# Layernorm, an S5 scan and a gated feed-forward on one core: first up-projection weights loaded and used by whole row tiles, with a new order of all steps

## The chip, the cores and the metric

The kernel runs on one core of a Trainium2 chip. The metric is the device time of one execution in microseconds (us), here the median of three runs: 179.26 before the change.

A core has five engines with a queue of instructions each: TensorE (PE, with the load of its stationary operand shown apart as PEld), VectorE (DVE), ScalarE (ACT), GpSimd (POOL) and SyncE (SP). An engine takes its instructions in the order in which they were written; across engines only semaphores set an order. Nearly all transfers of this kernel are issued by SP, some of them transposing on the way.

## The reference, cut to what matters

```python
def _A_ref(x, Lambda_re, Lambda_im, B_re, B_im, C_re, C_im, log_dt, Dskip):
    Lam = Lambda_re + 1j * Lambda_im
    dt = jnp.exp(log_dt)
    Lam_bar = jnp.exp(dt * Lam)
    B_bar = ((Lam_bar - 1.0) / Lam)[:, None] * Bmat
    Bu = jnp.einsum("bld,pd->blp", x + 0j, B_bar)
    for t in range(L):
        h = Lam_bar[None, :] * h + Bu[:, t, :]
    y = 2.0 * jnp.einsum("blp,dp->bld", hseq, Cmat).real + x * Dskip[None, None, :]

def _B_ref(x, w_gate, w_up, w_down):
    return (_gelu(x @ w_gate) * (x @ w_up)) @ w_down

xn = _layernorm(x, axis=-1)
return x + _A_ref(xn, ...) * _silu(_B_ref(xn, w_gate, w_up, w_down))
```

x is 2048 tokens by 512 in bf16, the state has 512 complex channels, and the feed-forward is 1376 wide.

## The kernel before

**Tiling.** The tokens are four slabs (s) of 512, each four token tiles (m) of 128. The model width is four row tiles (k) of 128. The 1376 columns of the up and gate weights are three chunks (c): 512, 512 and 352 columns. One PE group is the four matmuls over k that fill one PSUM bank for one token tile and one chunk; 16 KB of PSUM per partition are eight banks, six in a pool called `ps` and two in a pool called `pp`.

**The plan.** The kernel's functions don't issue anything directly. Each call puts a step (an engine, a function that emits the instructions, what it reads and writes) into a `Plan`; steps are numbered in the order of the calls. `Plan.run` then emits them in the order of the tuple `ORDER`, written out by hand, and a buffer's or bank's number for each use comes from `SLOTS`, also written out. Costs and due times in the calls ("end", "landed", "rank") play no part in what is emitted. So what the chip sees is, for each engine, the order of its own steps in `ORDER`, and for each buffer who used it last.

**The first slab (s = 0).** `load_x` (L296) and `load_w` (L287) issue the pieces on SP, in `ORDER`'s order: x0, x1, x2 and wu row tile 0, chunk 0; then single row tiles of chunks 0 and 1 of wu (128 KB each) with x3 among them, row tile 3 as 1024 columns, one block with the last 352 columns of all four row tiles, and two blocks of wg. Behind them come slab 1, the skip vector `Drow`, the B matrices by transposing DMA (`BT`), and so on.

`center` (L411 to L424) takes the mean off a token tile with ACT and DVE, `squares` (L428) sums the squares on ACT, and POOL makes the reciprocal deviation `rs`. The mean-free tile is transposed on PE by `head_t` (L387, L400; four transposes a tile) and copied by DVE to `xcT`, which lies in the scan's buffer W. Because `rs` is not yet known, the products are made of the unscaled tile, and ACT scales them while it copies them out of PSUM (`out_up`, L471; for the gate together with the gelu, L505).

`up_rows` (L462) issues a single matmul of an up group, for one m, k and c, so that PE can work on whichever row tile has arrived, with several banks open at once. It is used for chunks 0 and 1 of all token tiles, streaming by row tile. `first_w` (L499) issues a whole group of four; it makes chunk 2 of the up product and the three gate chunks of every token tile. `parameters` (L672, L673) transposes the step sizes and eigenvalues on PE with two small transposes; the DVE, POOL and ACT steps behind them (`angles`, `tables`) make the rotation tables `tab`.

**Later slabs.** ACT normalizes a token tile to `xna` (L843), a transposing DMA on SP makes `xnT` of four tiles (`dma_t4`, L436), and `gate_tile` (L536, copies L539) makes up and gate groups.

**What all slabs share.** The gated product (DVE, L518) overwrites `at`, SP transposes it into `atT` (`at_t`, L551), and `down_pair` multiplies it with `wd` (L564, 11 matmuls of 512 columns) and ACT puts a silu on it (L567). The scan is made in two halves (h) of the channels per slab: four PE groups per half multiply `BT` with `xnT` (L615), ACT copies them to U (L617), DVE rotates them with a table (`rot`, L627, and `turn`, L635 and L639), runs four scans (L646), carries the end state (L655 to L660) and rotates back into `hst`. `y_part` makes an output tile: ACT puts the skip part into a bank (L575), PE adds eight matmuls of `hst` and the scaled C matrices (L579), DVE multiplies by the silu (L585) and adds x (L586), and SP stores it (L589).

**The C matrices** come by two transposing DMAs into `CT` (L807), which lies in slab 1's `hst` buffer; for each of four pieces ACT makes `tF` (L809) and DVE two products (L811, L814) that form C2, the last of which has to stand before the first output product.

**ACT's tables.** Silu and sine stand in one table set and gelu in another; each change of the set that the order brings about puts an ACT_TABLE_LOAD ahead of the step.

**The SP queue in the middle.** Up to the first `atT` its order is: slab 1, `Drow`, `BT` real, xnT(0), `BT` imaginary, slab 2, wd's tail (L763), slab 3, xnT(1), wd (L762), C imaginary, `atT` of tiles 0 and 1 of slab 0, C real.

The two calls by which the change's head goes are these:

```python
        if (m, c) not in opened:
            opened[m, c] = bank(m == 3)
...
            T.matmul(ps[:], lhsT=xcT[:, k, m * P : (m + 1) * P], rhs=wu[:, k, a:b], start=(k == 0), stop=(k == KT - 1))
        pe(1, 512, f, [("xcT", m, k // 2), ("wu", k, c)], [key])
```

Of the kernel before, what the change touches and what calls it, by code (L numbers as in the profile page):

```python
# [51 lines left out]
    ),  # L52
    "pp": (
        0, 1, 0, 1, 0, 1, 0, 1, 0, 0, 0, 1, 0, 1, 0, 1, 0, 1, 0, 1, 1, 0, 1, 0, 1, 1, 1, 0, 0, 0, 0, 1, 1, 0, 1, 0, 1, 0, 1,
    ),
    "U": (
        0, 1, 0, 2, 0, 1, 0, 2,
    ),
    "g2": (
        5, 0, 1, 4, 3, 0, 4, 2, 2, 0, 1, 5, 3, 1, 4, 5,  # L60
    ),
    "at": (
        2, 0, 1, 3, 2, 1, 0, 0, 0, 1, 2, 3, 2, 3, 0, 1,
    ),
    "gtA": (
        0, 0, 1, 1, 0, 1, 0, 1, 1, 0, 0, 0, 1, 1, 0, 0,
    ),
    "gtB": (
        1, 1, 0, 0, 0, 0, 1, 1, 1, 0, 0, 0, 0, 1, 0, 1,
    ),  # L70
    "ubA": (
        0, 1, 0, 0, 1, 1, 1, 0, 0, 0, 1, 1,
    ),
    "ubB": (
        0, 0, 1, 1, 1, 0, 0, 1, 0, 0, 1, 0,
    ),
    "yg": (
        0, 0, 1, 1, 0, 1, 0, 1, 0, 1, 1, 0, 0, 0, 1, 0, 1, 0,
    ),
    "ot": (  # L80
        1, 1, 1, 0, 1, 0, 0, 0, 0, 0, 0, 1, 1, 0, 1, 0, 1,
    ),
    "sk": (
        2, 3, 0, 1, 5, 7, 4, 6, 0, 1, 3, 2, 5, 4, 6, 7,
    ),
    "atT": (
        0, 1, 3, 0, 1, 1, 3, 2, 0, 3, 2, 1, 1, 2, 3, 0,
# [61 lines left out]
def kernel(  # L149
# [18 lines left out]
    P = 128  # L168
    S = 2048
    D = 512  # L170
    F = 1376
# [129 lines left out]
    load_x(2, 2.06, 3.75)  # L301
    load_w("wu", 0, 1, 0, W1, 2.53, 4.4)
    load_w("wu", 0, 1, W1, W2, 3.0, 4.95)
    load_w("wu", 1, 2, 0, W1, 3.47, 5.5)
    load_w("wu", 1, 2, W1, W2, 3.94, 6.05)
    load_x(3, 4.41, 6.6)
    load_w("wu", 2, 3, 0, W1, 4.88, 7.15)
    load_w("wu", 2, 3, W1, W2, 5.35, 7.7)
    load_w("wu", 3, 4, 0, W2, 5.82, 8.8)
    load_w("wu", 0, KT, W2, F, 6.29, 10.0)  # L310
    load_w("wg", 0, KT, W1, F, 6.76, 12.4)
    load_w("wg", 0, KT, 0, W1, 7.23, 14.0)
    for ri, src in enumerate((A_B_re, A_B_im)):
        dma(SP, 2.0, 3.0, lambda ri=ri, src=src: nc.sync.dma_start_transpose(out=BT[:, ri, :, :], in_=src), writes=[("BT", ri)],
            after=list(sp_last), svc=TURN)
    ident = sb("ident", [P, P])
    pool(0.65, lambda: make_identity(nc, ident[:]), writes=["ident"], rank=600.0, not_before=0.72)
# [136 lines left out]
    def up_rows(m, k, c):  # L454

        a, b = CH[c]
        if (m, c) not in opened:
            opened[m, c] = bank(m == 3)
# [461 lines left out]
```

## Time and profile before

| what | us |
|---|---|
| runs | 178.82, 179.26, 179.27 |
| median | 179.26 |
| profiled execution, first to last instruction (its span) | 176.9 |
| mean granted TensorE clock | 1.000 of full speed |

No time of its own was taken for the profiled execution: it has the span alone, and the runs' times are taken around the whole launch, so the two differ by what lies ahead of the first and behind the last instruction. Where a time is predicted, that difference is taken as constant.

Busy time by stretch of the span (us; in brackets instructions), from the view of windows:

| window | PE | DVE | ACT | POOL |
|---|---|---|---|---|
| 0 to 7 | 6.12 (28) | 3.69 (18) | 4.95 (13) | 2.48 (12) |
| 7 to 16 | 8.95 (49) | 3.36 (13) | 7.24 (17) | 3.68 (9) |
| 31 to 71.2 | 39.99 (194) | 38.35 (70) | 39.53 (77) | 1.01 (1) |
| 173.8 to 176.9 | 0.00 (0) | 0.71 (2) | 0.00 (0) | 0.00 (0) |

How to read the rows below. Times are microseconds unless marked ns. `L499` is line 499 of the kernel; `bank<-wu,W` is output and inputs by the program's names (`xcT` appears as W, CT as `hst`). In the chain of waits each row is the start, the length, and the engine with its line: the chain is followed back from the last instruction to what released each step. In a time line a row is the start, the time from the first to the last of a run of equal instructions, the engine, the line, the operation, shapes and their count. A row of windows gives the window, its length, then busy time and count of PE, PEld, DVE, ACT and POOL, the granted clock, the busy share of the DMA engines and the KB per us (GB/s) that they moved. A DMA row gives the mean size and the median time from issue to landing. "issue" stands for time in which nothing that the profile shows was waited for.

### The profile page before, as it was taken

To read this page: it belongs to the slowest core of one execution; us is meant where nothing else is said; L and a number is where in the kernel's file an instruction comes from. 1 tells how busy PE (TensorE), PEld (TensorE's weight loads), DVE (VectorE), ACT (ScalarE), POOL (GpSimd) and SP (SyncE) were. 2 spreads that over 40 slices of the span, in tenths; PEclk is the share of its full clock that TensorE was granted. 3 is DMA by queue.
4 is the path that set the end of the run, shared out by engine and by line. 5 is a ranking of instruction groups with operands and counts; after the bars stand their busy time and mean duration, and the time that the engine had idled before them with its cause. 6 is when DMAs were issued, how large, how long until landed. Compare 5 with 4: busy or idle time off the path is not lost.

```text
span 176.9 us, 2418 instructions
## 1 busy us (share of the span) xinstructions
PE 172.1 (97%) x834; PEld 82.3 (47%) x849; DVE 154.6 (87%) x253; ACT 132.6 (75%) x246; POOL 10.9 (6%) x25
## 2 busy tenths in 40 slices
PE   8999999999999999999999999999999999999992
PEld 2554544454454444444444444444444444444451
DVE  3743799999999988999999699999999999999343
ACT  6679999989999999956697665735898860793310
POOL 2640500000200000011000000000000000000000
PEclk9999999999999999999999999999999999999999
DMA  5999999997092730040057050063007300550531
GB/s 150 285 347 247 160 288 189 305 217 158 8 193 43 138 62 4 0 82 0 0 115 150 2 111 0 0 126 70 0 11 154 87 0 4 129 123 0 113 119 30
DMA packets 48467, 18.66 MB, mean 105 GB/s; under 512 B 40296, under 2 KB 48328, under 8 KB 48456
## 3 DMA queue, kind: packets, MB, share of 16 engines
q1 hardware_dynamic: 48432, 18.52, 46.7%
q8 instruction: 6, 0.10, 0.2%
q14 instruction: 5, 0.04, 0.1%
q10 hardware_dynamic: 24, 0.00, 0.0%
HBM read 6.46 MB, written 2.10 MB: 48 GB/s over the span
## 4 chain that ended last, share of the span: by engine, by line
PE 94%; DMA 2%; SPq 1%; issue 1%; DVE 0%
PE bank L536 31%; PE bank L564 21%; PE bank L615 16%; PE bank L579 16%; PE bank L499 7%; PE bank L462 3%; DMA wu<-in_B_w_up_dram 2%; SPq L296 1%; SPq L287 0%; DVE yg L585 0%; DVE ot L586 0%; PE bank L400 0%
## 5 line engine op out<-in xcount | busy, mean ns | idle before, releaser
L536 PEld LDWEIGHTS <-xnT 128*128 128x128 bf16 x288 | 28.1, 98 | 29.4
L564 PE MATMUL bank<-wd,atT 128*128 128x512 bf16 (+1 forms) x174 | 40.2, 379 | 0.1
L536 PE MATMUL bank<-wu,xnT 128*128 128x512 bf16 (+1 forms) x140 | 31.9, 356 | 0.1
L536 PE MATMUL bank<-wg,xnT 128*128 128x512 bf16 (+1 forms) x139 | 31.7, 356 | 0.3
L615 PE MATMUL bank<-xnT,BT 128*128 128x512 bf16 x128 | 30.9, 379 | 0.1
L646 DVE TENSOR_TENSOR_SCAN Fs<-rho,ini,W 128x512 bf16<-128x512 f32 x24 | 29.8, 1272 | 0.1
L579 PE MATMUL bank<-C,hst 128*128 128x512 bf16 (+1 forms) x134 | 29.7, 366 | 0.1
L564 PEld LDWEIGHTS <-atT 128*128 128x128 bf16 (+1 forms) x176 | 17.2, 98 | 20.3
L539 ACT ACTIVATE ubA<-bank 128x512 bf16<-128x512 f32 x24 | 14.6, 614 | 8.8 <-PE bank L536 8.3
L617 ACT ACTIVATE U<-bank 128x512 bf16<-128x512 f32 x32 | 19.1, 622 | 1.7 <-PE bank L615 1.7
L579 PEld LDWEIGHTS <-hst 128*128 128x128 bf16 x136 | 13.3, 98 | 14.0
L615 PEld LDWEIGHTS <-BT 128*128 128x128 bf16 x128 | 12.5, 98 | 14.3
L627 DVE TENSOR_TENSOR Q<-U,tab 128x4096 bf16<-128x4096 bf16 x8 | 18.3, 2287 | 0.7 <-ACT tab L715 0.6
L539 ACT ACTIVATE gtA<-bank 128x512 bf16<-128x512 f32 x24 | 14.8, 616 | 5.3 <-PE bank L536 4.6
L627 DVE TENSOR_TENSOR Q<-Fs,tab 128x4096 bf16<-128x4096 bf16 x8 | 18.3, 2285 | 0.1
L567 ACT ACTIVATE g<-bank 128x512 f32<-128x512 f32 x16 | 9.2, 594 | 12.1 <-PE bank L564 12.1
L585 DVE TENSOR_TENSOR yg<-bank,g 128x512 bf16<-128x512 f32 (+1 forms) x17 | 11.1, 655 | 5.0 <-PE bank L579 4.6
L539 ACT ACTIVATE ubB<-bank 128x352 bf16<-128x352 f32 x12 | 5.7, 475 | 6.6 <-PE bank L536 5.5
L838 ACT ACTIVATE junk<-x_tok 128x512 bf16<-128x512 bf16 x16 | 10.2, 649 | 0.0
L499 PE MATMUL bank<-wg,W 128*128 128x512 bf16 (+1 forms) x47 | 9.7, 356 | 0.1
L843 ACT ACTIVATE xna<-x_tok,nb,rs 128x512 bf16<-128x512 bf16 x12 | 9.6, 876 | 0.0
L575 ACT ACTIVATE bank<-sk 128x512 f32<-128x512 bf16 (+1 forms) x17 | 9.5, 577 | 0.1
(121 smaller groups left out, 190.0 us busy)
## 6 DMA issues: line engine op xcount, KB each, us to landing
out_dram<-ot SPq DMA_DIRECT2D x15, 128.0 KB, 1.8
x_tok<-in_A_x_dram SPq DMA_DIRECT2D x3, 512.0 KB, 5.6
wd<-in_B_w_down_dram SPq DMA_DIRECT2D x1, 1280.0 KB, 7.1
wg<-in_B_w_gate_dram SPq DMA_DIRECT2D x1, 864.0 KB
wu<-in_B_w_up_dram SPq DMA_DIRECT2D x6, 128.0 KB, 3.3
x_tok<-in_A_x_dram SPq DMA_DIRECT2D x4, 128.0 KB, 2.2
wg<-in_B_w_gate_dram SPq DMA_DIRECT2D x1, 512.0 KB, 7.8
wu<-in_B_w_up_dram SPq DMA_DIRECT2D x1, 352.0 KB, 3.9
```

What stands on the lines that cost most here:

```text
L499: T.matmul(ps[:, 0 : b - a], lhsT=xcT[:, k, m * P : (m + 1) * P], rhs=wt[:, k, a:b], start=(k == 0), stop=(k == KT - 1))
L536: T.matmul(ps[:, 0 : b - a], lhsT=xnT[:, s % 2, m, k, :], rhs=wt[:, k, a:b], start=(k == 0), stop=(k == KT - 1))
L539: acts(b - a, lambda: act(out=dst, in_=ps[:, 0 : b - a], func=AF.Copy if up else AF.Gelu_apprx_tanh), [key], [ok], table=None if up else " ...
L564: T.matmul(ps[:], lhsT=atT[:fs, k, iT * P : (iT + 1) * P], rhs=wd[:fs, k, :], start=(k == 0), stop=(k == NFT - 1))
L579: T.matmul(ps, lhsT=hst[s % 2][:, j // NPT, j % NPT, m * P : (m + 1) * P], rhs=C2[:, j // NPT, j % NPT, c0:c1], start=False, stop=(j == 2 ...
L585: dve(w, lambda: V.tensor_tensor(out=yg[iy][:, 0:w], in0=ps, in1=g2[ig][:, c0:c1], op=ALU.mult), [key, ("g2", gg)], [("yg", gy)])
L615: T.matmul(ps[:], lhsT=BT[:, ri, k, pt * P : (pt + 1) * P], rhs=xnT[:, s % 2, :, k, :], start=(k == 0), stop=(k == KT - 1))
L617: acts(512, lambda q=q, ri=ri, ps=ps: act(out=U[ui][:, ri, q, :], in_=ps[:], func=AF.Copy), [key], [("U", ug, q, ri)])
L627: dve(4096, lambda: V.tensor_tensor(out=Qf, in0=src.unsqueeze(1).to_broadcast(WQ), in1=table, op=ALU.mult), reads, ["Q"], rate=2.0)
L646: pl.add(DVE, 1.12 if s == 0 else 1.185, lambda ri=ri, q=q, pt=pt, first=first: V.tensor_tensor_scan(out=Fs[:, ri, q, :], data0=rho[:, pt ...
L838: acts(512, lambda i=i, fn=fn, sc=sc, m=m: act(out=junk()[:], in_=x_tok[:, s * M + m, :], func=fn, scale=sc, accum_out=sx[:, s, i, m : m + ...
L843: acts(512, lambda m=m: act(out=xn[m], in_=x_tok[:, s * M + m, :], func=AF.Identity, scale=rs[:, s, m : m + 1], bias=nb[:, s, m : m + 1]), ...
```

## The change

**Loads.** Each row tile of wu now comes as two pieces, 512 columns and 864 columns (chunks 1 and 2 together), eight pieces in all; the block with the last 352 columns of all row tiles and the 1024-column piece are gone. In the program the call for x2 stands behind wu(0, chunk 0) and that for x3 behind wu(2, chunks 1 and 2). As `ORDER` issues them: x0, x1, x2, wu(0, 512), wu(0, 864), wu(1, 512), wu(1, 864), wu(2, 512), wu(2, 864), x3, wu(3, 512), wu(3, 864), wg, wg.

**Products of the first slab.** `up_rows` streams all three chunks of token tiles 0 and 1 and chunks 0 and 1 of tile 2, by row tile, and its matmul is as wide as its chunk. Chunk 2 of tile 2 and the whole of tile 3 are made by `first_w`. The banks of tile 2 come from the pool `pp` where those of tile 3 did. The number and the widths of all matmuls together stay the same.

**Orders.** `ORDER` and `SLOTS` are new from the first step to the last. Decoded by engine, what differs most is this.

- PE: the parameters' transposes stand right behind those of token tile 0 and ahead of those of tile 1; behind tile 2's transposes the up matmuls of all three chunks are mixed. Behind the streams come two up groups of tile 3, then gate groups with the last up groups between them: up (3, 0), up (3, 1), gate (0, 2), gate (3, 1), gate (1, 2), gate (3, 0), gate (0, 1), gate (2, 1), gate (3, 2), gate (2, 0), up (3, 2), gate (0, 0), gate (1, 1), the first Bu group, up (2, 2); the number pairs are token tile and chunk. The first output tile is (slab 0, tile 3) where it was (0, 2), with 242 matmuls of 512 columns ahead of it where there were 258.
- SP, behind the loads: slab 1, `Drow`, `BT` imaginary, xnT(0), `BT` real, slab 2, xnT(1), wd's tail, C imaginary, C real, slab 3, wd, then `atT` of slab 0 for tiles 3, 1, 2, 0.
- DVE: ahead of the last C2 piece stand one rotation, one carry and one small gated product less.
- ACT: the order calls for 19 changes of the table set where there were 15.

```diff
 ORDER = (
-    18, 23, 19, 17, 20, 22, 21, 29, 0, 24, 28, 16, 25, 1, 26, 2, 27, 3, 4, 30, 31, 11, 44, 32, 6, 33, 34, 46, 45, 7, 35, 5, 36, 50, 65, 47, 67, 69,
...
+    18, 16, 29, 24, 0, 1, 3, 25, 26, 2, 27, 30, 44, 31, 32, 33, 45, 46, 34, 35, 36, 38, 65, 39, 47, 19, 66, 67, 51, 50, 37, 4, 5, 6, 7, 8, 9, 10,
...
     load_x(0, 1.12, 2.92)
     load_x(1, 1.59, 3.35)
-    load_x(2, 2.06, 3.75)
-    load_w("wu", 0, 1, 0, W1, 2.53, 4.4)
-    load_w("wu", 0, 1, W1, W2, 3.0, 4.95)
-    load_w("wu", 1, 2, 0, W1, 3.47, 5.5)
-    load_w("wu", 1, 2, W1, W2, 3.94, 6.05)
-    load_x(3, 4.41, 6.6)
-    load_w("wu", 2, 3, 0, W1, 4.88, 7.15)
-    load_w("wu", 2, 3, W1, W2, 5.35, 7.7)
-    load_w("wu", 3, 4, 0, W2, 5.82, 8.8)
-    load_w("wu", 0, KT, W2, F, 6.29, 10.0)
-    load_w("wg", 0, KT, W1, F, 6.76, 12.4)
-    load_w("wg", 0, KT, 0, W1, 7.23, 14.0)
+    load_w("wu", 0, 1, 0, W1, 2.06, 3.85)
+    load_x(2, 2.53, 4.3)
+    load_w("wu", 0, 1, W1, F, 3.0, 5.3)
+    load_w("wu", 1, 2, 0, W1, 3.47, 5.75)
+    load_w("wu", 1, 2, W1, F, 3.94, 6.6)
+    load_w("wu", 2, 3, 0, W1, 4.41, 7.05)
+    load_w("wu", 2, 3, W1, F, 4.88, 7.9)
+    load_x(3, 5.35, 8.3)
+    load_w("wu", 3, 4, 0, W1, 5.82, 8.9)
+    load_w("wu", 3, 4, W1, F, 6.29, 9.9)
+    load_w("wg", 0, KT, W1, F, 6.76, 12.6)
+    load_w("wg", 0, KT, 0, W1, 7.23, 14.3)
...
         if (m, c) not in opened:
-            opened[m, c] = bank(m == 3)
+            opened[m, c] = bank(m == 2)
         key, ps = opened[m, c]
 
         def f():
-            T.matmul(ps[:], lhsT=xcT[:, k, m * P : (m + 1) * P], rhs=wu[:, k, a:b], start=(k == 0), stop=(k == KT - 1))
-        pe(1, 512, f, [("xcT", m, k // 2), ("wu", k, c)], [key])
+            T.matmul(ps[:, 0 : b - a], lhsT=xcT[:, k, m * P : (m + 1) * P], rhs=wu[:, k, a:b], start=(k == 0), stop=(k == KT - 1))
+        pe(1, b - a, f, [("xcT", m, k // 2), ("wu", k, c)], [key])
...
     head_t(1)
-    up_rows(0, 0, 0)
-    up_rows(0, 0, 1)
+    for m in range(2):
+        for c in range(3):
+            up_rows(m, 0, c)
     head_t(2)
-    for c in range(2):
-        up_rows(1, 0, c)
-    up_rows(0, 1, 0)
-    up_rows(1, 1, 0)
-    for c in range(2):
-        up_rows(2, 0, c)
-    for m in range(2):
-        up_rows(m, 1, 1)
-    for c in range(2):
-        up_rows(2, 1, c)
+    for k in range(1, KT):
+        for m in range(2):
+            for c in range(3):
+                up_rows(m, k, c)
+        if k == 1:
+            for c in range(2):
+                up_rows(2, 0, c)
+        for c in range(2):
+            up_rows(2, k, c)
     head_t(3)
-    for c in range(2):
-        for m in range(3):
-            up_rows(m, 2, c)
-    for k in range(3):
-        for c in range(2):
-            up_rows(3, k, c)
-    for m in range(M):
-        for c in range(2):
-            up_rows(m, 3, c)
-    for m in range(M):
-        first_w("wu", m, 2)
+    first_w("wu", 2, 2)
+    for c in range(3):
+        first_w("wu", 3, c)
```

More of the change, by code (lines that the diff above doesn't have):

```diff
@@ L48 @@
     "ps": (
[3 rows of a table removed]
[3 rows of a table added]
     ),
     "pp": (
-        0, 1, 0, 1, 0, 1, 0, 1, 0, 0, 0, 1, 0, 1, 0, 1, 0, 1, 0, 1, 1, 0, 1, 0, 1, 1, 1, 0, 0, 0, 0, 1, 1, 0, 1, 0, 1, 0, 1,
+        0, 0, 1, 0, 1, 0, 1, 0, 1, 1, 0, 1, 0, 0, 1, 1, 0, 0, 1, 1, 0, 0, 1, 0, 1, 1, 1, 1, 0, 0, 0, 0, 1, 0, 0, 0, 0,
     ),
     "U": (
-        0, 1, 0, 2, 0, 1, 0, 2,
+        0, 1, 2, 0, 1, 2, 0, 1,
     ),
     "g2": (
-        5, 0, 1, 4, 3, 0, 4, 2, 2, 0, 1, 5, 3, 1, 4, 5,
+        1, 3, 2, 0, 4, 1, 0, 5, 5, 1, 3, 2, 0, 2, 3, 4,
     ),
     "at": (
-        2, 0, 1, 3, 2, 1, 0, 0, 0, 1, 2, 3, 2, 3, 0, 1,
+        2, 1, 0, 3, 1, 2, 0, 3, 0, 2, 3, 1, 3, 2, 1, 0,
     ),
     "gtA": (
-        0, 0, 1, 1, 0, 1, 0, 1, 1, 0, 0, 0, 1, 1, 0, 0,
+        1, 0, 1, 0, 1, 1, 0, 0, 0, 1, 1, 0, 1, 0, 1, 1,
     ),
     "gtB": (
-        1, 1, 0, 0, 0, 0, 1, 1, 1, 0, 0, 0, 0, 1, 0, 1,
+        1, 0, 1, 0, 1, 0, 1, 1, 0, 1, 1, 1, 0, 0, 1, 1,
     ),
     "ubA": (
-        0, 1, 0, 0, 1, 1, 1, 0, 0, 0, 1, 1,
+        1, 1, 0, 1, 1, 1, 0, 0, 1, 1, 1, 0,
     ),
     "ubB": (
-        0, 0, 1, 1, 1, 0, 0, 1, 0, 0, 1, 0,
+        1, 0, 1, 0, 1, 0, 1, 0, 1, 1, 1, 0,
     ),
     "yg": (
-        0, 0, 1, 1, 0, 1, 0, 1, 0, 1, 1, 0, 0, 0, 1, 0, 1, 0,
+        0, 1, 1, 0, 0, 1, 0, 0, 1, 0, 0, 1, 0, 0, 1, 1, 1, 0,
     ),
     "ot": (
-        1, 1, 1, 0, 1, 0, 0, 0, 0, 0, 0, 1, 1, 0, 1, 0, 1,
+        0, 0, 1, 1, 1, 1, 1, 1, 1, 0, 0, 1, 1, 0, 0, 0, 1,
     ),
     "sk": (
-        2, 3, 0, 1, 5, 7, 4, 6, 0, 1, 3, 2, 5, 4, 6, 7,
+        1, 3, 2, 0, 6, 4, 7, 5, 1, 3, 0, 2, 5, 0, 4, 7,
     ),
     "atT": (
-        0, 1, 3, 0, 1, 1, 3, 2, 0, 3, 2, 1, 1, 2, 3, 0,
+        3, 1, 2, 0, 2, 0, 1, 3, 1, 0, 2, 3, 2, 0, 3, 1,
     ),
```

52 rows, old and new, of tables (ORDER, SLOTS) are left out of this document.

## The prediction

> **What bounds the kernel now.** I read the page first, then the chain of waits in order of time, then the time line of the start, and at last those of ScalarE (ACT) and of the SP queue.
>
> ```profile
> span 176.9 us, 2418 instructions
> ```
> ```profile
> PE 172.1 (97%) x834; PEld 82.3 (47%) x849; DVE 154.6 (87%) x253; ACT 132.6 (75%) x246; POOL 10.9 (6%) x25
> ```
> ```profile
> 3.06 3.89 DMA wu<-in_B_w_up_dram
> 6.95 0.04 issue
> 6.99 1.35 PE bank L499 x8
> ...
> 10.24 0.22 PE bank L400 x4
> ...
> 12.40 0.60 PE bank L499 x4
> ...
> 68.10 2.38 PE bank L564 x11
> ...
> 172.01 1.76 PE bank L579 x16
> ```
>
> From 6.99 to 173.77 us the chain is TensorE (PE) alone. Eleven matmuls of 512 columns take 2.38, so one is worth 0.216; four of 352 columns take 0.60, so one is worth 0.15; the four transposes of a token tile take 0.22. The change neither adds nor removes a matmul, so it can win only what PE stands still before 6.99, and it loses whatever new stop it brings behind. What stands behind 173.77, the last product's two DVE steps and its store, keeps its form.
>
> ```profile
> 5.21 0.40 PE L400 MATMUL bank<-ident,xna 128*128 128x128 bf16 x4
> 5.54 0.17 PE L672 MATMUL bank<-ident,pv 4*128 4x4 bf16 x1
> 5.58 0.16 PE L673 MATMUL bank<-ident,pv 8*128 8x8 bf16 x1
> 5.67 1.25 PE L462 MATMUL bank<-wu,W 128*128 128x512 bf16 x5
> 6.99 1.35 PE L499 MATMUL bank<-wu,W 128*128 128x352 bf16 x8
> ```
>
> **The head.** The transposes of token tile 2 start at 5.21; PE is free at 5.43. The next five matmuls start at 5.67, after the parameters' transposes, and at 0.216 apiece are done at 6.75; then PE waits for the 352-column block until 6.99. So 0.24 + 0.24 = 0.48 is lost. In the new order the parameters' transposes stand ahead of token tile 1's, at about 4.3, where PE waits for VectorE (DVE) anyhow, and the 352-column chunks no longer hang on one transfer. What goes is 0.45, if the new pieces land in time.
>
> ```profile
> 2.11 1.93 SPq L287 DMA_DIRECT2D wu<-in_B_w_up_dram  x4
> ```
> ```profile
> x_tok<-in_A_x_dram SPq DMA_DIRECT2D x4, 128.0 KB, 2.2
> ```
> ```profile
> 3.00:6.00 3.00, 2.95 (x20) 1.11 (x18) 2.57 (x10) 2.90 (x10) 0.36 (x2) 1.00 0.90 260
> 6.00:9.00 3.00, 2.94 (x18) 1.54 (x17) 2.25 (x10) 1.61 (x5) 2.67 (x6) 1.00 1.01 298
> ```
>
> SP issues four loads in 1.93, one each 0.475, and by the last column 260 to 298 KB/us arrive. The SP queue still begins with x0, x1, x2, wu(0, chunk 0): the calls are swapped, the order by which they are issued is not. The first new piece, 864 columns or 216 KB, is the fifth. The 352 KB load is issued at 3.06 as the sixth, and lands 3.89 later. The new fifth, issued at 2.58 with fewer bytes, lands at 4.4 (where wu(0, chunk 0) lands: issue at 2.11 plus the 2.2 of a 128 KB tile) plus 216/280 = 0.8, at 5.2; PE wants it at 5.43. The next pieces land 0.45 (128 KB) and 0.77 (216 KB) apart: 5.6, 6.4, 6.9, 7.6, x3 8.1, 8.6, 9.3. PE, counted through its new order, wants them at 6.1, 7.1, 7.4, 8.4, 9.2 and 10.5. The cover is 0.2 for the first piece and 0.5 to 1.2 for the others; gone, it costs what lands late, one for one. I take 0, and up to 0.6 for the range (the third rival).
>
> **ACT's evictions.** PSUM banks are reused as the new slots say, and a matmul group into a used bank waits for ACT's copy out of it.
>
> ```profile
> 9.93 0.71 ACT L428 ACTIVATE junk<-x_tok,ma 128x512 bf16<-128x512 bf16 x1
> ```
> ```profile
> 13.09 0.55 ACT L471 ACTIVATE at<-bank,rs 128x352 bf16<-128x352 f32 x1 [0.19 <-issue]
> ```
> ```profile
> 13.74 1.83 ACT L471 ACTIVATE at<-bank,rs 128x512 bf16<-128x512 f32 x3
> 15.59 1.28 ACT L505 ACT_TABLE_LOAD   x1
> 16.88 0.69 ACT L505 ACTIVATE gtA<-bank,rs 128x512 bf16<-128x512 f32 x1
> ```
> ```profile
> 22.94 2.94 ACT L843 ACTIVATE xna<-x_tok,nb,rs 128x512 bf16<-128x512 bf16 x4
> ```
> ```profile
> 16.00:31.00 15.00, 14.95 (x76) 7.26 (x75) 13.73 (x26) 14.70 (x27) 2.76 (x3) 1.00 1.07 217
> ```
> ```profile
> 71.20:173.80 102.60, 102.08 (x494) 48.96 (x501) 94.78 (x127) 66.13 (x116) 1.01 (x1) 1.00 0.28 60
> ```
>
> Three copies take 1.83, the last of them 0.69: they follow each other every 0.57, 0.12 less than one lasts (so 0.45 or less for 352 columns, which last 0.55); four normalizations take 2.94. From 16 to 31 ACT is busy for 14.70 of 15.00, and PE stays ahead only because each bank it asks for has just been emptied. The new order makes that worse. PE: from 5.48 (tile 2's transposes) 23 matmuls of 512 and 8 of 352 and four transposes, 6.4, to 11.86; two up groups of tile 3 (2 x 0.86), then gate groups (0.60, 0.86, 0.60, 0.86), to 16.50, where gate (tile 0, chunk 1) asks for the bank of gate (3, 1). ACT: its run of copies can start at 11.1, since the cosine ahead waits for DVE; 512, 352, a square (0.71), 352, 512 and 512 columns, to 14.5; the load of the gelu table, 1.28; gate (3, 1) to 16.54. So PE stops for 0.10. Next is tile 2's gate chunk 1 at 17.5, which waits for the copy of up (3, 1), 0.12. At 26.0 gate (1, 0) waits for a copy that stands behind the four normalizations (2.94), 0.12, and the next Bu group another 0.07. At 34.3 an up group of slab 1 waits for a Bu copy that stands behind five sums of slab 2, 0.22. Together 0.63; each comes out of a count of 15 to 25 ACT steps, so 0.2 to 1.2 holds it. I take 0.65.
>
> Counted along the new order ACT changes tables 19 times, where before it is 15: 4 x 1.28 = 5.1 more. All four lie behind 71 us, where ACT is idle for 102.6 - 66.1 = 36.5; there they cost nothing unless a bank hangs on them. Four groups between 73 and 152 keep margins of only 0.1 to 0.25 by my count, for which I add 0.1 (0 to 0.5).
>
> The trace has the first copy behind the load at 16.88, 1.29 after 15.59. [...]
>
> **The SP queue between 25 and 50 us.** Before, the queue runs xnT(1), wd, C_im, two atT, C_re. Now it runs xnT(1), wd's tail, C_im, C_re, slab 3, wd, atT of tile 3, then the other three.
>
> ```profile
> 25.91 2.98 SPq L436 DMA_TRANSPOSE xnT<-xna  x1
> 28.94 0.59 SPq L762 DMA_DIRECT2D wd<-in_B_w_down_dram  x1
> 29.57 6.21 SPq L807 DMA_TRANSPOSE hst<-in_A_C_im_dram  x1
> 35.88 3.13 SPq L551 DMA_TRANSPOSE atT<-at  x2
> 39.06 1.86 SPq L807 DMA_TRANSPOSE hst<-in_A_C_re_dram  x1
> ```
> ```profile
> wd<-in_B_w_down_dram SPq DMA_DIRECT2D x1, 1280.0 KB, 7.1
> ```
> ```profile
> atT<-at SPq DMA_TRANSPOSE x16, 3.5
> ```
>
> wd is issued at 28.94 and lands 7.1 later, at 36.0; the transpose behind it holds SP until 35.78. A transpose behind a big copy thus is stuck until the copy is nearly in. Before, the C transpose stood there; now the first atT does. Its time: xnT(1) is issued at 25.5 (ACT's fourth normalization ends 0.4 earlier) and takes 2.98, to 28.5; the tail 0.5; the two C transposes 1.9 to 2.5 each, to 32.8 to 34.0; slab 3 adds 512 KB ahead of wd, 1.3 to 2.1 at 250 to 400 KB/us; wd 7.1. So wd lands at 41.2 to 43.2 and atT some 2.1 behind (3.5 less the 1.4 that an unhindered issue holds SP): 43.3 to 45.3.
>
> Who waits: DVE's gated product of slab 1, tile 3, which overwrites the buffer that this atT reads. By a count of its steps DVE reaches it at 43.8, and all its later work is queued behind.
>
> ```profile
> 67.31 2.29 DVE L627 TENSOR_TENSOR Q<-U,tab 128x4096 bf16<-128x4096 bf16 x1 [0.64 <-ACT tab L715]
> 69.52 0.74 DVE L811 SCALAR_TENSOR_TENSOR C<-hst,cre,tF 128x512 bf16<-128x512 bf16 x1
> ```
> ```profile
> 71.18 1.89 PE L579 MATMUL bank<-C,hst 128*128 128x512 bf16 x8
> ```
>
> Its due date: the first output product (L579) needs the last of the C2 pieces. Before, that ends at 70.26 and the product starts at 71.18, 0.9 later. In the new order 16 matmuls of 512 fewer stand ahead of the first product (242 for 258): 3.45 earlier, 0.45 earlier from the head, 0.65 later from ACT, so about 67.9. DVE has one rotation (2.2), one carry (0.4) and one small gated product (0.25) less ahead of that piece: 67.4. That leaves 0.4, the wait at 43.8 takes it from 44.2 on, and past it PE loses one for one (at 60.8 a gate group whose bank a silu must empty, then at the product). With atT at 43.3 the loss is 0, at 45.3 it is 1.1; the middle, 44.3, and DVE's usual small waits put it at 0.35.
>
> **Sum.** The profiled execution has a span of 176.9; 2.4 lie around it if it took the median 179.26 (runs: 178.82 to 179.27), and the change touches nothing there. -0.45 + 0.65 + 0.10 + 0.35 = +0.65: a span of 177.5, **179.9**.
>
> **Rivals.** (1) The queue is in time: atT lands before 44.2, and -0.45 + 0.65 + 0 to 0.1 is left, 179.5. For it: 44.2 is inside the bounds. Against: every slip goes one way. (2) The other side, not slower: ACT is never late. It decides at the gate (3, 1) copy: if that ends by 16.4, with the table's load overlapping as at 15.59, the later copies are 0.2 earlier too, all five stops go, and the head's gain stays: 178.8. Against: ACT's 14.70 of 15.00. (3) The loads are late: 864-column rows arrive like the 352-column block, 352 KB from about 4.8 to 6.95, 165 KB/us. Then 216 KB take 1.3, and the pieces come at 5.7, 7.3, 8.9, 10.9; the stops add to 0.6: 180.5. For it: that row; against: 260 to 298 KB/us over the whole stretch. (4) wd is later than 43.2, atT at 45.8, the loss 1.6: 181.1.
>
> **How the numbers follow.** What a measurement of this kernel can tell from no change is about 0.3%, 0.54 us. Forecast 0.37, rivals 0.28, 0.12, 0.13, 0.10. Slower by more than 0.54: most of the forecast (0.33) and of the third and fourth (0.22), 0.55. Faster: half of the second, 0.06. Within: 0.39. The range 178.8 to 181.2 holds all but the ends; the forecast's own is 179.5 to 180.6.
>
> **What would show it.** The 0.24 before 6.99 is gone, and the 352-column up matmuls lie between the others. In the list of waits PE, which now waits for nobody, has ACT behind it at 16 to 18, 26 and 34. The first atT lands at 43.3 to 45.3 and DVE idles before it. Wrong it is if PE's rows run on without a break (rival 2), if SP's copies are not what holds the first atT, or if a stop of over 0.5 stands at a place that I don't name.

## The result, and the profile after

The changed kernel takes 181.67 us (median of four runs, 181.46 to 181.93) against 179.04 (178.76 to 179.27) before: 1.015 times the time, interval 1.013 to 1.017. It is slower, as forecast, but by 2.6 where 0.65 was forecast, and lies above the range.

The chain of waits by engine, before:

```profile
PE 94%; DMA 2%; SPq 1%; issue 1%; DVE 0%
```

The page of the changed kernel, then its list of what PE waited for (in all, times, longest):

```profile
span 180.0 us, 2418 instructions
...
PE 173.2 (96%) x833; PEld 82.4 (46%) x849; DVE 155.0 (86%) x253; ACT 137.9 (77%) x250; POOL 10.4 (6%) x25
...
PE 46%; DVE 32%; ACT 12%; issue 5%; DMA 3%; SPq 0%; ACTq 0%; DVEq 0%
```
```profile
PE bank L564 <- ACT gtA L539: 1.0, 1, 1.0
PE bank L375 <- PEq L896: 0.8, 1, 0.8
PE bank L499 <- ACT gtA L505: 0.7, 1, 0.7
```

The chain is no longer PE alone. Where it now runs through DVE, PE is mostly busy as well, as the windows below show. (The row with L375 is the start of the kernel and is the same before.) The windows answer to those of before:

```profile
16.00:31.00 15.00, 14.29 (x70) 6.79 (x70) 12.82 (x40) 14.99 (x29) 2.51 (x4) 1.00 0.95 177
...
71.20:173.80 102.60, 101.15 (x482) 47.73 (x489) 96.12 (x125) 74.29 (x125) 1.01 (x1) 1.00 0.29 58
```

From 16 to 31 PE is busy for 14.29 where it was for 14.95, and behind 71 us for 101.15 of 102.60.

To place every loss, I went through PE's steps: the start of the next one, less the start of this one, less what this one's matmuls take at full speed (0.2158 per 512 columns, 0.149 per 352, 0.054 per transpose, by the rows of before). What is left is called a **stop** here; it also counts matmuls that run slower. Summed over the trace that is 1.24 before and 4.35 after, 3.11 more; the last product starts 3.08 later (175.80 for 172.72). PE's stops by stretch, in us, with every kernel of this study:

| kernel | to 16 | 16 to 45 | 45 to 140 | 140 on | all | time, us |
|---|---|---|---|---|---|---|
| before | 1.12 | 0.01 | 0.07 | 0.04 | 1.24 | 179.04 |
| before again (e10) | 1.60 | 0.01 | 0.07 | 0.04 | 1.72 | 179.22, one run |
| changed | 1.34 | 1.50 | 0.34 | 1.17 | 4.35 | 181.67 |
| changed again (e11) | 1.70 | 1.48 | 0.10 | 1.17 | 4.44 | 181.88, one run |
| e1, tiny gelu early | 1.57 | 0.54 | 0.50 | 1.18 | 3.80 | 180.88 |
| e2, one wait less | 1.25 | 0.57 | 0.32 | 1.18 | 3.32 | 180.73 |
| e3, tiny gelu late | 1.01 | 1.49 | 0.10 | 0.07 | 2.67 | 180.65 |
| e4, atT first | 1.60 | 1.50 | 0.10 | 1.17 | 4.38 | 181.80 |
| e5, e2 + e3 + e4 | 1.57 | 0.57 | 0.10 | 0.06 | 2.30 | 179.84 |
| e6, e5 + split piece | 1.38 | 0.51 | 0.10 | 0.04 | 2.02 | 179.67 |
| e7, e6 + two moves | 0.96 | 0.49 | 0.10 | 0.04 | 1.58 | 179.51 |
| e12, e7 without split | 1.99 | 0.43 | 0.10 | 0.06 | 2.58 | 179.53 |
| e8, before, parameters first | 1.61 | 0.01 | 0.07 | 0.04 | 1.73 | 178.84 |
| e9, before, row 1 first | 2.54 | 0.01 | 0.07 | 0.04 | 2.66 | 180.06 |

In the changed kernel the 16 to 45 column is 0.82 at 17.95, 0.16 at 18.97, 0.15 at 27.55, 0.07 at 28.48 and 0.30 at 36.02; the 45 to 140 column is 0.13 at 62.45, 0.12 at 74.83 and what any kernel has; the last is 1.14 at 153.54.

### The profile page after: what moved, and what is told of

Same layout as the page of the kernel before. It is cut to its first block, busy times and chain, and to the rows that moved or that the text cites. A ratio compares the mean times of both kernels' runs of the same rounds, so it can differ in the third digit from the quotient of the medians.

```text
span 180.0 us, 2418 instructions
## 1 busy us (share of the span) xinstructions
PE 173.2 (96%) x833; PEld 82.4 (46%) x849; DVE 155.0 (86%) x253; ACT 137.9 (77%) x250; POOL 10.4 (6%) x25
## 4 chain that ended last, share of the span: by engine, by line
PE 46%; DVE 32%; ACT 12%; issue 5%; DMA 3%; SPq 0%; ACTq 0%; DVEq 0%
PE bank L564 14%; PE bank L536 14%; DVE Fs L646 10%; PE bank L579 10%; DVE Q L627 9%; PE bank L615 4%; DVE hst L639 3%; ACT gtA L505 3%; PE bank L462 2%; DVE at L518 2%; DVE W L639 2%; DVE yg L585 2%; DMA wu<-in_B_w_up_dram 2%; PE bank L499 2%; ACT junk L830 2%
## 5 line engine op out<-in xcount | busy, mean ns | idle before, releaser
L564 PE MATMUL bank<-wd,atT 128*128 128x512 bf16 (+1 forms) x171 | 39.6, 379 | 1.2 <-ACT gtA L539 1.0
L536 PE MATMUL bank<-wu,xnT 128*128 128x512 bf16 (+1 forms) x141 | 31.1, 356 | 0.2
L579 PE MATMUL bank<-C,hst 128*128 128x512 bf16 (+1 forms) x132 | 28.7, 366 | 0.2
L539 ACT ACTIVATE ubA<-bank 128x512 bf16<-128x512 f32 x24 | 14.1, 599 | 3.4 <-PE bank L536 3.4
L539 ACT ACTIVATE gtA<-bank 128x512 bf16<-128x512 f32 x24 | 14.2, 613 | 3.0 <-DVE at L518 2.6
L499 PE MATMUL bank<-wg,W 128*128 128x512 bf16 (+1 forms) x47 | 10.2, 356 | 0.7 <-ACT gtA L505 0.7
L830 ACT ACTIVATE junk<-x_tok 128x512 bf16<-128x512 bf16 x16 | 10.7, 687 | 0.0
```

Of the source, the lines that this page charges most:

```text
L499: T.matmul(ps[:, 0 : b - a], lhsT=xcT[:, k, m * P : (m + 1) * P], rhs=wt[:, k, a:b], start=(k == 0), stop=(k == KT - 1))
L536: T.matmul(ps[:, 0 : b - a], lhsT=xnT[:, s % 2, m, k, :], rhs=wt[:, k, a:b], start=(k == 0), stop=(k == KT - 1))
L539: acts(b - a, lambda: act(out=dst, in_=ps[:, 0 : b - a], func=AF.Copy if up else AF.Gelu_apprx_tanh), [key], [ok], table=None if up else " ...
L564: T.matmul(ps[:], lhsT=atT[:fs, k, iT * P : (iT + 1) * P], rhs=wd[:fs, k, :], start=(k == 0), stop=(k == NFT - 1))
L579: T.matmul(ps, lhsT=hst[s % 2][:, j // NPT, j % NPT, m * P : (m + 1) * P], rhs=C2[:, j // NPT, j % NPT, c0:c1], start=False, stop=(j == 2 ...
L830: acts(512, lambda i=i, fn=fn, sc=sc, m=m: act(out=junk()[:], in_=x_tok[:, s * M + m, :], func=fn, scale=sc, accum_out=sx[:, s, i, m : m + ...
```

## The experiments: a table load behind a wait

The two largest stops look alike. The time lines of ACT and of PE in the changed kernel, at 17.95:

```profile
13.10 1.71 ACT L471 ACTIVATE at<-bank,rs 128x352 bf16<-128x352 f32 x3
15.91 1.28 ACT L505 ACT_TABLE_LOAD   x1 [1.11 <-PE bank L499]
17.21 0.69 ACT L505 ACTIVATE gtA<-bank,rs 128x512 bf16<-128x512 f32 x1
```
```profile
17.95 3.51 PE L499 MATMUL bank<-wg,W 128*128 128x512 bf16 x16 [0.66 <-ACT gtA L505]
```

ACT is free at 14.81. The load's row names nothing that it reads, yet it stands still for 1.11, until PE's group is done, and only then takes its 1.28. In before the same load started at once (15.59, behind 13.74 + 1.83), though the last matmul of the group that its copy reads began only at 15.64. The copy behind the load has two waits outstanding in the changed kernel, for PE's group and for POOL's rs of token tile 3, which no ACT step has read yet; in the trace the copy carries one of them, and the other, PE's, stands ahead of it as a semaphore instruction of its own (it ends at 15.88), and ahead of the load, too. In before that copy was of tile 1, whose rs an earlier copy had waited for, and PE's wait stood on the copy alone.

**e1** lets the load start without a wait; **e2** takes one of the two waits away and leaves the load where it was.

```diff
+        def copy():
+            if (m, c) == (3, 1):
+                act(out=tiny[:], in_=one, func=AF.Gelu_apprx_tanh)                 # e1
+                act(out=tiny[:], in_=rs[:, 0, m : m + 1], func=AF.Copy)            # e2, in its place
+            act(out=dst, in_=ps[:, 0 : b - a], func=AF.Gelu_apprx_tanh, scale=rs[:, 0, m : m + 1])
+        acts(b - a, copy, [key, ("rs", 0, m)], [gk], ptr=1, table="gelu", rank=80.0 - 10 * m)
```

> The changed kernel with one tiny gelu on ScalarE, which reads a constant and so waits for nothing, ahead of the copy of gate (3, 1). Theory A: in the changed kernel this copy has two outstanding waits (PE's group and POOL's rs), one of them is put ahead of the table load, and so the load of 1.28 us starts only when PE is done, at 15.91; with the tiny gelu the load starts when the up copies end, at about 14.8, the copy follows PE's group at once, and PE's stop at 17.3 to 17.95 shrinks from 0.82 to about 0.1: the span falls by 0.7, the time from 181.67 to about 181.0. Theory B: ScalarE is full there in any case (14.99 of 15.00 us from 16 to 31), the stop reappears within the next groups: PE's sum of stops by 31 us falls by less than 0.2 and the time stays at 181.5 or above.

> The changed kernel with one tiny copy (no table of its own) on ScalarE that reads rs of token tile 3 ahead of the copy of gate (3, 1); it takes POOL's wait, so that the gelu behind it has PE's wait alone. Theory A (the load is put behind one of two waits): the load carries no wait, starts at about 15.0, and the gain is that of the tiny gelu, 0.6 to 0.7 us: about 181.0. If instead a load always waits with its step, it starts at 15.9 as before and the time stays at 181.7. Theory B (ScalarE is full): 181.5 or above, with the stop moved to later groups.

Measured: 180.88 (180.62 to 181.20) and 180.73 (180.50 to 180.85). The time line of ACT, e1 and then e2:

```profile
13.37 1.71 ACT L471 ACTIVATE at<-bank,rs 128x352 bf16<-128x352 f32 x3
15.09 1.28 ACT L508 ACT_TABLE_LOAD   x1
16.39 0.20 ACT L508 ACTIVATE tiny<-const-float32-1.0 128x1 f32<-128x1 f32 x1
16.50 0.67 ACT L509 ACTIVATE gtA<-bank,rs 128x512 bf16<-128x512 f32 x1
```
```profile
14.74 0.22 ACT L508 ACTIVATE tiny<-rs 128x1 f32<-128x1 f32 x1
14.98 1.28 ACT L509 ACT_TABLE_LOAD   x1
16.28 0.69 ACT L509 ACTIVATE gtA<-bank,rs 128x512 bf16<-128x512 f32 x1
```

In both the load follows its neighbour at once, and the stop of 0.82 is gone, with the next three behind it (0.16, 0.15, 0.07): 16 to 45 falls from 1.50 to 0.54 and 0.57. Theory A holds, and e2 says which half of it counts: with one wait the load runs ahead by itself, at 14.98, where the last matmul of its copy's group begins at 15.45. Theory B falls, by the window of e1:

```profile
16.00:31.00 15.00, 14.90 (x76) 7.17 (x74) 13.47 (x46) 14.99 (x31) 2.92 (x4) 1.00 0.96 181
```

ACT is as full as ever, 14.99, and PE works for 14.90. It was not how much ACT does, but when one load may start. What is left of the stretch are 0.26 (e1) and 0.42 (e2) at 23.1, where the first Bu group waits for xnT(0), and 0.24 and 0.10 at 35.

The second place, ACT, DVE and PE of the changed kernel:

```profile
147.77 1.28 ACT L567 ACT_TABLE_LOAD   x1
149.42 0.60 ACT L567 ACTIVATE g<-bank 128x512 f32<-128x512 f32 x1 [0.36 <-PE bank L564]
151.60 1.28 ACT L539 ACT_TABLE_LOAD   x1 [1.58 <-DVE at L518]
152.90 0.60 ACT L539 ACTIVATE gtA<-bank 128x512 bf16<-128x512 f32 x1
```
```profile
150.84 0.68 DVE L518 TENSOR_TENSOR at<-gtA,ubA 128x1024 bf16<-128x1024 bf16 x1
```
```profile
153.54 2.54 PE L564 MATMUL bank<-wd,atT 128*128 128x512 bf16 x11 [0.97 <-ACT gtA L539]
```

Gate (3, 0) of slab 3 writes a buffer that DVE's gated product reads until 151.52, and it reads PE's bank: two waits again, and the load of 1.28 starts behind DVE's. The load at 147.77 shows the other case: its copy has one wait, for PE, and the load is over at 149.05, before PE's group ends at 149.38. Leaving out the load at the program's start, only the two at 15.91 and 151.60 of the changed kernel's 19 have idle time of more than 0.02 ahead of them; of the 15 of before none has. One load of before, at 110.01, has a semaphore ahead of it as well; that one was passed at 109.42, while ACT was still at work, and cost nothing. **e3** puts a tiny gelu ahead of the copy of gate (3, 0), in the same way as e1.

```diff
+            def copy():
+                if (s, m, nm, c) == (3, 3, "wg", 0):
+                    act(out=tiny[:], in_=one, func=AF.Gelu_apprx_tanh)
+                act(out=dst, in_=ps[:, 0 : b - a], func=AF.Copy if up else AF.Gelu_apprx_tanh)
+            acts(b - a, copy, [key], [ok], table=None if up else "gelu")
```

> The changed kernel with one tiny gelu on ScalarE ahead of the copy of gate (3, 0) of slab 3. Theory A: there the load is put behind the wait for VectorE's gated product (151.52) and the copy ends at 153.49, where PE stands from 152.57 on; with the load done at about 151.3 the copy ends at about 152.15, PE's stop of 1.14 goes, and the time falls by 1.1 to about 180.6. Theory C: the gated product itself, late on VectorE, is what PE hangs on; then PE still stops at this place or at the next group, and at most 0.4 is won: 181.3 or above.

Measured: 180.65 (180.16 to 181.27), 1.0 less. ACT in e3:

```profile
149.48 1.28 ACT L542 ACT_TABLE_LOAD   x1
150.78 0.20 ACT L542 ACTIVATE tiny<-const-float32-1.0 128x1 f32<-128x1 f32 x1
151.07 0.60 ACT L543 ACTIVATE gtA<-bank 128x512 bf16<-128x512 f32 x1
```

The load lies in what was ACT's idle time, the copy follows DVE, and the column "140 on" falls from 1.17 to 0.07. Theory C falls: the product itself was in time.

## The experiments: the SP queue

**e4** puts slab 3 and wd behind the first two atT on SP (steps 438 and 152 behind 177).

```diff
-    ..., 142, 438, 152, 179, 177, ...
+    ..., 142, 179, 177, 438, 152, ...
```

> The changed kernel with the first two atT transposes (token tiles 3 and 1 of slab 0) ahead of slab 3 and wd on SP. Theory D: the transposes stuck behind wd cost VectorE 0.3 to 0.4 at 47.6 to 47.95, and through the sums of slab 2 and a silu PE's stop of 0.13 at 62.4; they now land at about 38 and 41, this idle time and this stop go, and 0.1 to 0.15 us is won (181.5). Rival: VectorE has other waits that take its place (the silu's table load at 60.5), or wd, which lands some 3 us later, holds the first down product; then the time stays at 181.7 or rises.

Measured: 181.80 (181.22 to 182.00), no gain that the time shows. SP and DVE of the changed kernel, then DVE of e4:

```profile
35.68 0.51 SPq L754 DMA_DIRECT2D wd<-in_B_w_down_dram  x1
36.29 12.37 SPq L551 DMA_TRANSPOSE atT<-at  x4
```
```profile
45.29 0.66 DVE L518 TENSOR_TENSOR at<-gtA,ubA 128x1024 bf16<-128x1024 bf16 x1
...
47.95 0.34 DVE L518 TENSOR_TENSOR at<-gtB,ubB 128x352 bf16<-128x352 bf16 x1 [0.33 <-DMA atT<-at]
```
```profile
47.73 0.33 DVE L515 TENSOR_TENSOR at<-gtB,ubB 128x352 bf16<-128x352 bf16 x1
```

The first atT lands at 44.87, before DVE comes to it at 45.29, which by then is late itself; it is the second, which lands at 47.93, that DVE waits for. In e4 they land at 38.92 and 40.54, and the wait is gone. But the changed kernel's second profile (e11) has no such wait either: there the second atT landed at 46.16 by itself. Over all profiles it fits: where the second atT landed late (changed 47.93, e1 47.34, e2 46.95; DVE idle for 0.33, 0.48, 0.28) the stretch from 45 to 140 has 0.34, 0.50 and 0.32 of stops; where it landed at 45.65 (e3) or 46.16, or was moved (e4, e5), it has 0.10. So Theory D names the cause, as far as seven profiles that agree can show it, and it costs 0.2 to 0.4 in some executions and nothing in others; the time of e4 alone can't tell.

**e5** joins e2, e3 and e4.

> The changed kernel with the three edits together: the tiny copy that takes POOL's wait ahead of gate (3, 1)'s copy, the tiny gelu ahead of gate (3, 0) of slab 3, and the first two atT ahead of slab 3 and wd. Theory (the stops are independent and each has its own cause): PE's stops by the trace fall by 0.9 + 1.14 + 0.25 = 2.3 from the changed kernel's 4.35, of which the head keeps 0.8 to 1.6 by how its loads land; the time is 179.4 (179.1 to 179.8). Rival: what is won early is lost at a later bound (VectorE, or PE's stops at 61 to 74), and the sum of gains is under 1.7: 180.0 or above.

Measured: 179.84 (179.27 to 180.05), just above what was given, and below the rival's 180.0. The stops fell by 2.05 from 4.35: the three causes by 2.28, as expected (0.57, 0.10 and 0.06 are left), while the head has 1.57. The window behind 71 us in e5:

```profile
71.20:173.80 102.60, 102.60 (x501) 48.70 (x499) 95.67 (x126) 74.04 (x123) 1.01 (x1) 1.00 0.29 60
```

PE is without a break, with all four additional table changes still there. By themselves they cost nothing.

## The experiments: the head

**e6** splits wu(0, 864) into 512 and 352 columns and lets PE take what is there first; **e7** adds two moves: the first Bu group (step 186) behind two more groups, and one sum of slab 2 (step 296) behind the Bu copy that PE wants at 35.

```diff
-    load_w("wu", 0, 1, W1, F, 3.0, 5.3)
+    load_w("wu", 0, 1, W1, W2, 3.0, 4.9)
+    load_w("wu", 0, 1, W2, F, 3.0, 5.3)
...
-    PE: (0,0,2) (0,0,1) (1,0,0) (1,1,0) (2,0,0) (2,0,1) (2,1,0) (1,0,1) (0,1,2) (1,0,2)
+    PE: (0,0,1) (1,0,0) (1,0,1) (2,0,0) (2,0,1) (0,0,2) (1,1,0) (2,1,0) (1,0,2) (0,1,2)
```

(The triples are m, k, c.)

> As the one with three edits, and wu row tile 0's 864-column piece split into 512 and 352 columns, with PE's first ten up matmuls in another order, so that the 512 columns come first. Theory E: the stop at the first up matmul of chunk 1 or 2 (0.1 to 0.9 in five profiles) comes from the 864-column piece landing at 5.4 to 6.3, where the 512-column piece of before landed at 4.84; the 512 columns now land at about 4.9 to 5.1, and PE's stops before 11 us fall to 0.6 to 0.9: 0.3 to 0.5 less, about 179.0. Rival: the loads are late together, because the bytes ahead of them are (260 to 300 KB per us); the stop moves to the next pieces, each now issued 0.47 later, and the head's stops stay at 1.2 to 1.6: 179.4.

> As the one before it (three edits and the head), and two steps moved: the first Bu group behind two more up and gate groups (it waited until 22.97 for xnT(0)), and one sum of slab 2 behind the Bu copy that PE waits for at 35. Theory: both stops (0.26 to 0.42 and 0.10 to 0.24) go, PE's stops between 16 and 40 fall below 0.2, the time falls by 0.4 to about 178.6, below before. Rival: ScalarE is full there, and another bank is late in their place; then 16 to 40 keeps 0.4 or more, and the time is that of the kernel without the moves.

Measured: 179.67 (179.40 to 180.02) and 179.51 (179.26 to 179.91), against 178.95 of before on the same chip (ratios 1.0041 and 1.0035, intervals 1.0028 to 1.0054 and 1.0023 to 1.0048). The 512 columns now land at 5.18 and 5.05 and the stop at the first matmul of a further chunk is gone in both; e6 still has 1.38 because x2 landed at 4.20 there. Of e7's moves both stops went, but a new one of 0.37 stands at 26.5, where gate (1, 0) waits for an ACT copy: 16 to 45 keeps 0.49. The rival is right there, and no version of the changed kernel got below before. What e7 still loses by the traces is 0.48 from 16 to 45 and 0.16 behind the last store, whose landing is followed by 1.0 to the end in e6 and e7 and by 0.83 in the kernels with one load less; why, no run shows. The two make 0.64, for 0.56 between the medians.

**e12** is e7 without the split.

> The three edits and the two moved steps, without the split of the 864-column piece, and so with as many loads as the changed kernel. If the split is worth 0.4 on PE (stops of 0.9 to 1.4 before 11 us with it, 0.8 to 1.6 without) and costs 0.17 behind the last product (the last store's landing to the end took 1.03 with it and 0.87 without, in the profiles), this one comes out 0.1 to 0.2 slower than the 179.51 of its twin: 179.6 to 179.7. If the head's stops are chance only, it is 0.17 faster: 179.35.

Measured: 179.53 (179.26 to 181.16, ten runs), between the two figures, so it doesn't decide what the split is worth in the median. (Before had 179.10 on that chip: ratio 1.0032, interval 1.0009 to 1.0056.) Its profile has the longest head of the changed versions, 1.99: wu(0, 864) landed at 6.70.

**e8** moves only the parameters' transposes, in the kernel before (step 38 ahead of 65). **e9** in addition issues both pieces of row tile 1 ahead of x3 and the 352-column block, puts PE's row 1 ahead of the first 352-column groups, and moves tile 3's centring on ACT and its transposes on PE to fit.

```diff
-    SP: wu(0, 512:1024), block of 352, wu(1, 512:1024), x3, wu(1, 0:512), ...
+    SP: wu(0, 512:1024), wu(1, 512:1024), wu(1, 0:512), x3, block of 352, ...
```

> The kernel before, with only the parameters' transposes moved ahead of token tile 1's. By the prediction's sum this alone would be worth 0.2 (178.8). Theory F: it is worth nothing by itself, since PE then reaches the 352-column block, which lands at 6.95, 0.2 earlier and waits 0.2 longer: 179.04 within 0.1, and PE's stop ahead of the first 352-column group grows from 0.24 to about 0.45.

> The kernel before with the head mended in its own pieces: the parameters' transposes ahead of token tile 1's, wu's row tile 1 (both 128 KB pieces) issued ahead of x3 and of the 352-column block, and PE's row 1 matmuls ahead of the first 352-column groups (on ScalarE the centring of tile 3 ahead of the first up copies). Theory F: the block of 352 KB, which lands at 6.95 to 7.4, is what PE waits for; row 1 lands at about 6.0 and 6.5, the block at about 8.0 and PE wants it then at 8.0; PE's stops before 11 us fall from 1.1 to 1.6 to 0.7 to 1.0: 0.3 to 0.5 less, 178.6, the first version below before. Rival: ScalarE, which copies the first three up groups 0.9 later, passes that on to the full stretch from 16 to 31, and PE stops there for as much: 179.0.

e8: 178.84 (178.58 to 179.18) against 178.95, ratio 0.9990 (0.9973 to 1.0006): no gain clear of noise, but the interval holds both Theory F's nothing and the 0.2 of the sum. The trace is on Theory F's side, since PE still waits for the block; the stop ahead of the block is 0.22 and not 0.45, though, because PE itself came there late (half speed, below). e9 is a miss: 180.06, ratio 1.007 (1.005 to 1.009). Row 1 came when expected (5.79 and 6.45, PE unbroken from 5.45 to 7.6), but the block took from x3's landing at 6.78 to 9.23, 352 KB in 2.45, and PE stood for 1.65. The block was slow wherever it stood: in the three other profiles of before's loads it took 1.6 to 2.6 behind the piece ahead of it.

**e10** and **e11** profile both kernels once more.

> The kernel before, unchanged, profiled once more, for its head: in its first profile PE's stops before 11 us were 1.12, in that of the kernel before with the parameters moved 1.60, where the 352-column block landed at 7.42 for 6.95 and PE ran its first matmuls at half speed until 6.3. If loads and PE's speed differ from one execution to the next by chance, this profile has 1.1 to 1.6, too; if the first profile shows what the kernel always does, it has 1.1 within 0.1.

> The changed kernel, unchanged, profiled once more: the stops at 17.9 (0.82), 19.0 (0.16), 27.5 (0.15), 28.5 (0.07), 36.0 (0.30) and 153 (1.14) come back to within 0.05, since they hang on ScalarE's order alone; the head's (1.34 before 11.2 us in the first profile) lies anywhere between 0.8 and 1.6, and those at 62 and 74 (0.13, 0.12) may come or not.

The chain of waits at the start, e11 and then e10:

```profile
2.59 3.82 DMA wu<-in_B_w_up_dram
6.41 0.04 issue
6.46 3.65 PE bank L462 x18
```
```profile
3.06 4.40 DMA wu<-in_B_w_up_dram
7.46 0.04 issue
```

Before's first profile was a lucky one: its block landed at 6.95, here at 7.46, and the head has 1.60 for 1.12. The changed kernel's head went from 1.34 to 1.70, and its stops from 16 us on came back one by one (0.82, 0.16, 0.15, 0.07, 0.29, 1.13).

## Why the prediction was wrong, by its own steps

**The bound** was right: PE unbroken from 6.99, so that there is at most the head to win and every new stop is lost one for one. Stops (+3.11) and the last product's start (+3.08) agree.

**The head, -0.45.** Failed. Two profiles of before have 1.12 and 1.60, two of the changed kernel 1.34 and 1.70, and over the eight profiles with the changed head the mean is 1.50: nothing won. The step that fell is the landing of the pieces, above all of the first, "plus 216/280 = 0.8, at 5.2". In those eight profiles it landed at 5.37 to 6.70, on average at 6.04, which is 0.9 to 2.3 behind the piece ahead of it. That is the third rival's mechanism, taken at 0.13, but for this piece alone: the second piece of 864 columns came 0.88 behind its neighbour on average, near the 0.77 of the sum.

In the first profile the first piece, at 5.66, happened to cost nothing, since x2 was late, too: it landed at 4.26 (3.81 in before), so that tile 2's transposes started at 5.51 (a stop of 0.30). And SP issued wu(2, 512) only at 4.27, because that transfer uses x2's semaphore again and waits for x2's landing; it landed at 7.95, where the sum had 6.9 (a stop of 0.29). The prediction has neither. The parameters' 0.2 can be won only where no load is waited for behind them; in before PE waited for the block in all three profiles (0.24, in e10 0.30, in e8 0.22). I had also taken a single profile's head as what the kernel always does.

**ACT's evictions, +0.65.** The five places and what stands behind each were right, and four sizes are near: 0.16 for 0.12, 0.15 for 0.12, 0.07 for 0.07, 0.30 for 0.22. For the first three of the four that is luck: they hang on the first stop, and in e1 and e2, where the load starts as the prediction had it, none of them is there, but a stop of 0.26 and 0.42 at xnT(0) that it doesn't name. The first is 0.82 for 0.10 (whose own terms, 14.5 + 1.28 + 0.69, make 16.47, which is no stop at all). The failed step is "the load of the gelu table, 1.28; gate (3, 1) to 16.54": it let the load start when ACT was free, as at 15.59 of before, though PE's group was done only at 15.9. e1 and e2 show it: there the stop is 0.05 and 0.06. The second rival, which hoped for an overlapped load at just this place, named the point that decides, but not what decides it.

**The tables, +0.10 (0 to 0.5).** That additional loads cost nothing unless a bank hangs on one is right (e5). That one would hang, for 1.14, was outside the bounds; the prediction doesn't name its four groups, so that it can't be told whether this is one of them. The step that failed is the same, a load taken to wait for nothing. This mechanism makes both misses, 0.72 in the first stop and 1.04 here: 1.76 of the 2.46 by which the stops exceed the forecast.

The load took 1.28 at both places, and the copy starts 1.30 behind the load's start (15.91 to 17.21, 151.60 to 152.90); the prediction's row of before has 1.29.

**The SP queue, +0.35.** SP held by wd until the first atT could be issued: right (36.29 to 41.6); its landing, 44.87, in the bounds. The price was 0.24 in that profile and nothing in the next, and it came by the second atT and a small product at 47.6, not by the first atT, which landed in time. (The sum's slack, 67.9 less 67.4, is 0.5 and not 0.4.) The first output product (69.5) had no stop.

**In sum,** by the first profile of each kernel: the head +0.22 for -0.45 (0.67 more), ACT 1.49 for 0.65 (0.84), the tables 1.14 for 0.10 (1.04), SP 0.24 for 0.35 (-0.11). That is 2.44 of the 2.46 between the forecast's 0.65 and the stops' 3.11. The runs' medians are only 2.6 apart, for before's first profile was a quick one (span 176.9, in e10 177.4).

## What to carry to other kernels

Where a new order puts a table change ahead of an activation, count the semaphores that this activation still has to wait for. In this kernel, with one, the load ran ahead of the data (14.98 in e2, 147.77 in the changed kernel); with two, it started behind one of them (15.91 and 151.60), and its 1.28 us were added to the path. (Whether the program's translation or the chip puts that wait ahead of the load, no run here shows.) A tiny step ahead that takes one of the waits, or the load itself, costs 0.2 (0.20 to 0.22 in e1, e2 and e3) and takes this away. And a head of a few us that hangs on transfers needs several profiles before a gain of 0.4 in it is written into a sum.

## What the runs showed of the hardware that I had not expected

PE's first matmuls run at half speed, until a moment that differs from one execution to the next. The same matmul of 512 columns in the changed kernel, and in before's second profile:

```profile
4.99 0.38 PE L462 MATMUL bank<-wu,W 128*128 128x512 bf16 x1
```
```profile
4.89 0.63 PE L462 MATMUL bank<-wu,W 128*128 128x512 bf16 x1
```

Each matmul of 512 columns that it catches costs some 0.2 more (in before's first profile two follow each other by 0.42 at 2.85 and by 0.22 at 6.33, in e8 by 0.43 at 5.85 and by 0.21 at 6.59). The clock column reads 1.00 for these first us, too, and so does the mean of 1.000 before; but the trace's clock records begin only at the moment at which the matmuls get faster, 4.48 in before's first profile and 4.99 in the changed kernel's, and what lies ahead has none. In the time lines the moment shows by the four transposes of a token tile, which take 0.40 behind it (at 4.60 in before's first profile, at 5.51 in the changed kernel's): in before's second profile they still take 0.61 at 4.49 and 0.63 at 5.31, while in e6 those at 3.79 take 0.54 and those at 4.52 already 0.40. PE is busy from 0.76 on in the first profiles of both kernels. What sets the moment, no run shows.
